# A Fourier filter and a two-layer network in one kernel: a table loaded with its negated columns, filter pieces cut elsewhere, and a last block that ends in parts

## The chip, the cores and the metric

The kernel runs on one core of a Trainium2 chip. The time is device microseconds of one execution; three runs of the kernel before gave 795.63, 795.70 and 795.91 us, median 795.7. One more execution was profiled.

The engines are TensorE (PE, matmuls; PEld its weight loads), VectorE (DVE), ScalarE (ACT), GpSimd (POOL) and SyncE (SP). DMAs are issued by instructions of SP, POOL or ACT and run beside the engines.

## The reference

```python
X = np.fft.rfft(x, axis=1)                 # x: 8 samples, 3008 positions, 256 channels
Y = X * (filt_r + 1j * filt_i)[None]       # 1505 frequencies, 256 channels
y = np.fft.irfft(Y, n=3008, axis=1)
h = y.reshape(24064, 256) @ w_in           # 256 x 2048
g = np.maximum(h, 0) + alpha * np.minimum(h, 0)
out = g @ w_out                            # 2048 x 256
```

## The kernel before

**The transform.** 3008 = 47 x 64, and the transform of a sample goes through in pieces. Piece a is a transform of length 47; then the data are turned; piece b multiplies by a table of twiddles (`twf_s`) for two of 24 frequencies k1 at a time (kp = 0 to 11 takes k1 = 2 kp and 2 kp + 1), VectorE multiplies the result by the filter (`filt_s`, L288 for sample 0), piece c multiplies by the inverse table (`twi_s` and `twx_s`), ScalarE or VectorE evicts to `v`; after another turn piece d ends in `yT`, the input of the network.

**Sample 0** has nothing to run beside, and is a class of its own (`First`). Its turns are done on PE (`turn_at`, L276, and `piece_t`, L312). Its piece b makes two products of 128 columns each per k1, from columns 64 to 192 and 0 to 128 of the table. The table `twf_s` in SBUF has 192 columns per k1; the constant in memory has 128, and the third part (128 to 192) is the first one negated, made on the chip by `third` (L327 on ScalarE, L329 on VectorE) for six k1 at a time. The two inverse tables have 128 partitions each, of which one half is loaded by SP (`load_twi`) and the other half is copied from it by POOL (`both_halves`, L341 and L342). `twx_s` lies in the last three buffers of `gtb`.

**POOL's order in sample 0** is written out by hand: the 8 loads of x, table columns for k1 0 to 6 (L332), filter pieces 0 to 4 (four DMAs, L142 and L146 for the real and the imaginary part), table 6 to 12, filter 4 to 10, table 12 to 18, filter 10 to 17, halves 0 to 4, table 18 to 24, filter 17 to 24, halves 4 to 8 and 8 to 12, the weights `win_s`, halves 12 to 18 and 18 to 24, the weights `wout_s`, the x of sample 1. POOL's DMAs share eight semaphores in turn, and a DMA is issued when the one eight places before it has landed.

**PE's order in sample 0**: for each kp, piece b of kp + 2, `turn_at` of kp + 4, piece c of kp - 2 (and 7, 8 and 9, 10 and 11 at the end). Piece b writes one of two PSUM buffers (`hps`), piece c one of two others (`op`).

**The network** runs in 48 blocks of 512 (some 384) positions, 16 steps each. A step j makes two matmuls of `up` (L452), on odd steps ScalarE evicts (L458) and VectorE makes the leaky rectifier (L461, L462) into a pair of `g`; beside it the same step makes `down` matmuls (L471) of the block before: 64 per block, row group by row group (128 positions, 16 matmuls of 256 columns each). After two row groups ScalarE evicts (L476) and SP stores (L434). The transforms of samples 1 to 7 are put between the steps by a plan of step numbers. The last block has no successor, so its 64 `down` matmuls run alone at the end.

Of the kernel before, what the change touches and what calls it, by code (L numbers as in the profile page):

```python
# [11 lines left out]
FP32 = mybir.dt.float32  # L12
# [3 lines left out]
N2 = 64  # L16
NK1 = 24
D = 256
# [14 lines left out]
AF = mybir.ActivationFunctionType  # L33
OP = mybir.AluOpType


def _build_consts():

    s1 = np.arange(N1)
    s2 = np.arange(N2)
    k1 = np.arange(NK1)
    p = np.arange(64)
    k2 = np.where(p < 32, p, 95 - p)
    g = np.where(p < 32, 1.0, -1.0)

    a1 = 2 * np.pi * np.outer(s1, k1) / N1  # L50
    wf1 = np.zeros((2 * N1, 96))
    wi3 = np.zeros((96, 2 * N1))
    scale = np.where(k1 == 0, 1.0, 2.0) / NFFT
    for h in range(2):
        r = slice(h * N1, h * N1 + N1)
        wf1[r, h * 48 : h * 48 + NK1] = np.cos(a1)
        wf1[r, h * 48 + NK1 : h * 48 + 48] = -np.sin(a1)
        wi3[h * NK1 : h * NK1 + NK1, r] = (np.cos(a1) * scale).T
        wi3[48 + h * NK1 : 48 + h * NK1 + NK1, r] = (-np.sin(a1) * scale).T

    kk = k1[:, None] + 47 * k2[None, :]
    ang = 2 * np.pi * s2[:, None, None] * kk[None, :, :] / NFFT
    c, s = np.cos(ang), np.sin(ang)
    twf = np.empty((128, NK1, 128))
    twf[:64, :, 64:], twf[64:, :, 64:] = c, s
    twf[:64, :, :64], twf[64:, :, :64] = -s * g, c * g
    ec, es = c.transpose(2, 1, 0), s.transpose(2, 1, 0)
    gp = g[:, None, None]
    twi = np.empty((128, NK1, 128))
    twi[:64, :, :64], twi[:64, :, 64:] = ec, es  # L70
    twi[64:, :, :64], twi[64:, :, 64:] = -es * gp, ec * gp
    return wf1, wi3, twf, twi
# [3 lines left out]
def kernel(  # L76
# [9 lines left out]
):  # L86
    nc = tc.nc
    wf1_np, wi3_np, twf_np, twi_np = _build_consts()
    wf1_d = nc.inline_tensor(wf1_np.astype(np.float16), name="c_wf1")
    wi3_d = nc.inline_tensor(wi3_np.astype(np.float16), name="c_wi3")  # L90
    twf_d = nc.inline_tensor(twf_np.astype(np.float16), name="c_twf")
# [10 lines left out]
    p_osb = ctx.enter_context(tc.tile_pool(name="p_osb", bufs=3))  # L102
    psH = ctx.enter_context(tc.tile_pool(name="psH", bufs=2, space=bass.MemoryType.PSUM))
    psO = ctx.enter_context(tc.tile_pool(name="psO", bufs=2, space=bass.MemoryType.PSUM))
# [9 lines left out]
    twf_s = konst.tile([128, NK1, 192], FP16, name="twf_s")  # L114
    twi_s = konst.tile([128, NK1, 128], FP16, name="twi_s")
# [7 lines left out]
    wout_s = konst.tile([128, 16, D], FP16, name="wout_s")  # L123
# [3 lines left out]
    twx_s = gtb[:, 14:17].rearrange("p a b c -> p (a b c)").rearrange("p (k m) -> p k m", m=128)  # L127
# [12 lines left out]
    def load_filt(dst, pbase, src, ka, kb):  # L140
        n = kb - ka
        nc.gpsimd.dma_start(  # L142
            out=dst[pbase : pbase + 32, ka:kb],
            in_=bass.AP(tensor=src.tensor, offset=src.offset + ka * D,
                        ap=[[47 * D, 32], [D, n], [1, D]]))
        nc.gpsimd.dma_start(  # L146
            out=dst[pbase + 32 : pbase + 64, ka:kb],
            in_=bass.AP(tensor=src.tensor, offset=src.offset + (N1 - ka) * D,
                        ap=[[47 * D, 32], [-D, n], [1, D]]))
# [171 lines left out]
    nc.sync.dma_start(out=wi3_s, in_=wi3_d.ap())  # L321
    make_identity(nc, id32)

    def third(eng, ka, kb):
        o, i = twf_s[:, ka:kb, 128:192], twf_s[:, ka:kb, 0:64]
        if eng is nc.scalar:
            nc.scalar.activation(o, i, AF.Copy, scale=-1.0)  # L327
        else:
            nc.vector.tensor_scalar(o, i, -1.0, None, OP.mult)  # L329

    def load_twf(ka, kb):
        nc.gpsimd.dma_start(out=twf_s[:, ka:kb, 0:128], in_=twf_d.ap()[:, ka:kb])  # L332

    def load_twi(ka, kb, ev):
        ev(twi_s[0:1, ka, 0:1], id16[0:1, 0:1])
        ev(twx_s[64:65, ka, 0:1], id16[64:65, 0:1])
        nc.sync.dma_start(out=twi_s[0:64, ka:kb], in_=twi_d.ap()[0:64, ka:kb])
        nc.sync.dma_start(out=twx_s[64:128, ka:kb], in_=twi_d.ap()[64:128, ka:kb])

    def both_halves(ka, kb):  # L340
        nc.gpsimd.tensor_copy(twi_s[64:128, ka:kb], twi_s[0:64, ka:kb])  # L341
        nc.gpsimd.tensor_copy(twx_s[0:64, ka:kb], twx_s[64:128, ka:kb])  # L342

    def load_g(ka, kb):
        load_filt(filt_s, 0, filt_r, ka, kb)
        load_filt(filt_s, 64, filt_i, ka, kb)

    load_twf(0, 6)
    load_g(0, 4)
    load_twf(6, 12)  # L350
    load_g(4, 10)
    load_twf(12, 18)
    load_g(10, 17)

    def warm(n):
        pw = psO.tile([128, 2, D], FP32, name="op")
# [11 lines left out]
            load_twi(4, 12, on_act)  # L368
    alp = psO.tile([128, 2, D], FP32, name="op")
    nc.tensor.transpose(alp[:, 0, 0:16], al16, id32)  # L370
    third(nc.scalar, 0, 6)
    f0.turn_at(0, on_act)
    f0.turn_at(1, on_dve)
    nc.vector.tensor_copy(al_s, alp[:, 0, 0:16])
# [1 line left out]
    f0.piece_b(0)  # L376
    f0.turn_at(2, on_act)
    f0.piece_b(1)
    both_halves(0, 4)
    load_twf(18, 24)  # L380
    load_g(17, 24)
    both_halves(4, 8)
    both_halves(8, 12)
    for kt in range(2):
        nc.gpsimd.dma_start(out=win_s[:, kt], in_=moe_w_in[kt * 128 : (kt + 1) * 128])
    third(nc.scalar, 6, 12)
    f0.turn_at(3, on_act)
    for kp in range(12):
        if kp < 10:
            if kp in (3, 6):  # L390
                third(nc.vector, 2 * kp + 6, 2 * kp + 12)
            f0.piece_b(kp + 2)
        if kp < 8:
            f0.turn_at(kp + 4, on_act)
        if kp == 0:
            load_twi(12, 24, on_act)
            both_halves(12, 18)
            both_halves(18, 24)
        for k in {9: (7, 8), 10: (9, 10), 11: (11,)}.get(kp, (kp - 2,) if kp > 1 else ()):
            f0.piece_c(k, on_dve if k == 10 else on_act)  # L400
    for q in range(2):
        nc.gpsimd.dma_start(
            out=wout_s[:, 8 * q : 8 * q + 8],
            in_=moe_w_out[1024 * q : 1024 * q + 1024].rearrange("(j p) d -> p j d", p=128))
# [15 lines left out]
    for p in range(NB // 2):  # L420
        t = 0
# [1 line left out]
            blocks.append((p, t, tn, 2 * p + (n >= 6)))  # L423
            t += tn

    def store(p, t0, osb, lane):
        t = t0
        while t < t0 + 128:
            b, r = 2 * p + t // NFFT, t % NFFT
            blk, o = r // 376, r % 376  # L430
            n = min(t0 + 128 - t, 376 - o)
            g, h = blk // 2, blk % 2
            row = b * NFFT + (o // 8) * N2 + NH * h + 8 * g
            nc.sync.dma_start(  # L434
                out=bass.AP(tensor=out.tensor, offset=out.offset + row * D,
                            ap=[[N2 * D, n // 8], [D, 8], [1, D]]),
                in_=osb[t - t0 : t - t0 + n, lane])
            t += n

    turn = [0]  # L440
# [1 line left out]
    class Block:  # L442
# [22 lines left out]
        def down(self, q):  # L465
            n = self.tn // 128
            for w in range(n * q, n * (q + 1)):
                si, k = w // 16, w % 16
                if si % 2 == 0 and k == 0:
                    self.op = psO.tile([128, 2, D], FP32, name="op")  # L470
                nc.tensor.matmul(self.op[:, si % 2], self.gts[k][:, 128 * si : 128 * si + 128],  # L471
                                 wout_s[:, k], start=(k == 0), stop=(k == 15))
                if k == 15 and (si % 2 == 1 or si == n - 1):
                    m = si % 2 + 1
                    osb = p_osb.tile([128, 2, D], FP32, name="osb")
                    nc.scalar.activation(osb[:, 0:m], self.op[:, 0:m], AF.Copy)  # L476
                    for lane in range(m):
                        store(self.p, self.t0 + 128 * (si - m + 1 + lane), osb, lane)

    plan = {}  # L480

# [36 lines left out]
    for b in range(3, NB):  # L518
        p = 96 * (b - 1)
# [19 lines left out]
    prev = None  # L539
    step = 0  # L540
    for p, t0, tn, _ in blocks:
# [6 lines left out]
                prev.down(j)  # L548
            step += 1
        prev = blk  # L550
    for q in range(16):
        prev.down(q)
    assert not plan


# [28 lines left out]
```

## Time and profile before

| | |
|---|---|
| median of three runs | 795.7 us |
| the profiled execution | 795.17 us |
| its span, first to last instruction | 793.4 us |
| PE, DVE, ACT, POOL busy | 97%, 78%, 75%, 25% |
| TensorE clock granted | 1.00 |
| first matmul of the network (L452) | 37.91 us |
| last matmul of the last block ends | 788.74 us |

Timeline rows read: start, length, engine, line, operation, tiles, shapes, count, and in brackets the idle time before and what ended it. Rows of the chain are start, length, what. Rows of the table by stretches are the stretch, its length, then busy time of PE, PEld, DVE, ACT and POOL with counts, the clock, the DMA share and GB/s. Times are in us from the start of the span.

### The profile page before, as it was taken

How to read it: one execution, taken by the hardware profiler on the slowest of the kernel's cores; microseconds unless marked ns; L12 is line 12 of the kernel's file. 1: busy time of each engine (PE TensorE's matmuls, PEld its weight loads, DVE VectorE, ACT ScalarE, POOL GpSimd, SP SyncE). 2: the span in 40 equal slices, each digit the busy share in tenths (PEclk: the TensorE clock that was granted, in tenths of full speed). 3: DMA queues.
4: the chain of work that ended last, by engine and by line, in shares of the span. 5: the costliest groups of instructions: out<-in, count | busy, mean ns of one | idle time of the engine just before them, and what ended most of it. 6: DMA issues, size and time to landing. Idle time of an engine off the chain costs nothing.

```text
span 793.4 us, 16044 instructions
## 1 busy us (share of the span) xinstructions
PE 773.1 (97%) x5908; PEld 538.5 (68%) x5908; DVE 619.8 (78%) x1368; ACT 597.9 (75%) x841; POOL 198.3 (25%) x275
## 2 busy tenths in 40 slices
PE   6899999999999999999999999999999999999997
PEld 6756656666676666766667666766667666766665
DVE  4787985788788787888787877887878888777773
ACT  4688778878778887788768887688867777787663
POOL 7710441153123221341223311242212222000000
PEclk9999999999999999999999999999999999999999
DMA  9995557685676648474684657656484333511111
GB/s 174 188 205 157 113 111 177 197 163 129 149 174 112 137 104 212 103 146 100 149 192 80 135 121 165 155 106 138 104 201 100 66 79 81 138 37 28 42 40 53
DMA packets 102517, 100.37 MB, mean 127 GB/s; under 512 B 11352, under 2 KB 92904, under 8 KB 102312
## 3 DMA queue, kind: packets, MB, share of 16 engines
q1 hardware_dynamic: 79992, 69.59, 33.2%
q0 software_dynamic: 22448, 29.77, 24.1%
q8 instruction: 46, 0.75, 0.4%
q14 instruction: 31, 0.25, 0.1%
HBM read 55.67 MB, written 46.66 MB: 129 GB/s over the span
## 4 chain that ended last, share of the span: by engine, by line
PE 88%; ACT 3%; DMA 3%; POOL 1%; DVE 1%; issue 1%; SPq 0%; ACTq 0%; POOLq 0%; DVEq 0%
PE hps L452 39%; PE op L471 39%; PE psF L175 3%; PE psF L236 3%; PE psF L214 2%; PE psF L195 2%; ACT gtb L458 2%; DMA twf_s<-c_twf 1%; DMA uu<-ww 1%; DMA filt_s<-in_filt_i_dram 1%; PE psF L312 1%; ACT asb L243 1%; POOL xs L137 1%; DMA zt<-v_dram 0%; DVE m L461 0%
## 5 line engine op out<-in xcount | busy, mean ns | idle before, releaser
L458 ACT ACTIVATE gtb<-hps 128x1024 f16<-128x1024 f32 (+1 forms) x384 | 385.3, 1004 | 133.4 <-PE hps L452 128.7
L471 PE MATMUL op<-wout_s,gtb 128*128 128x256 f16 x3008 | 451.1, 272 | 0.6 <-DVE gtb L462 0.6
L452 PE MATMUL hps<-yT,win_s 128*128 128x512 f16 (+1 forms) x1536 | 449.2, 374 | 0.4 <-ACT gtb L458 0.2
L471 PEld LDWEIGHTS <-gtb 128*128 128x128 f16 x3008 | 293.3, 98 | 189.5 <-DVE gtb L462 0.9
L461 DVE TENSOR_SCALAR m<-gtb,alm_s 128x512 f16<-128x512 f16 (+1 forms) x768 | 235.4, 349 | 126.7 <-ACT gtb L458 124.2
L462 DVE TENSOR_TENSOR gtb<-gtb,m 128x1024 f16<-128x1024 f16 (+1 forms) x384 | 261.6, 681 | 20.2 <-PE hps L452 0.5
L201 POOL DMA_DIRECT2D uu<-ww x168 | 140.3, 976 | 444.4 <-PE hps L452 307.9
L452 PEld LDWEIGHTS <-win_s 128*128 128x128 f16 x1536 | 145.2, 98 | 30.9 <-issue 3.1
L243 ACT ACTIVATE asb<-psF 96x512 f16<-96x512 f32 x112 | 66.2, 591 | 11.5 <-PE psF L175 11.4
L243 ACT ACTIVATE yT<-psF 128x376 f16<-128x376 f32 x120 | 57.1, 485 | 13.2 <-PE psF L236 12.7
L476 ACT ACTIVATE osb<-op 128x512 f32<-128x512 f32 x96 | 56.2, 585 | 6.1 <-issue 3.2
L198 DVE TENSOR_TENSOR ww<-psF,filts_s 128x512 f16<-128x512 f32 x84 | 57.4, 684 | 0.0
L243 ACT ACTIVATE v<-psF 128x512 f16<-128x512 f32 x84 | 49.4, 596 | 10.6 <-PE psF L214 9.8
L199 DVE TENSOR_TENSOR uu<-psF,filt_s 128x512 f16<-128x512 f32 x84 | 57.2, 681 | 0.0
L137 POOL DMA_DIRECT2D xs<-in_x_dram x64 | 44.4, 974 | 20.0 <-PE psF L175 14.0
L175 PE MATMUL psF<-xs,wf_s 94*96 94x512 f16 x112 | 42.7, 381 | 1.5 <-ACT v L243 0.9
L236 PE MATMUL psF<-wi_s,zt 96*128 96x94 f16 x504 | 40.3, 204 | 1.8 <-DMA zt<-v_dram 0.9
L236 PEld LDWEIGHTS <-zt 96*128 96x128 f16 x512 | 34.3, 97 | 6.1 <-issue 1.5
L214 PE MATMUL psF<-uu,twi_s 128*128 128x256 f16 x168 | 31.3, 273 | 2.3 <-DMA uu<-ww 1.3
L195 PE MATMUL psF<-at,twf_s 128*128 128x256 f16 x168 | 32.1, 272 | 0.3 <-ACT asb L243 0.2
L214 PEld LDWEIGHTS <-twi_s 128*128 128x128 f16 x168 | 15.7, 98 | 6.1 <-issue 2.0
L195 PEld LDWEIGHTS <-twf_s 128*128 128x128 f16 x168 | 15.8, 98 | 2.6 <-DVE uu L199 0.4
(59 smaller groups left out, 177.2 us busy)
## 6 DMA issues: line engine op xcount, KB each, us to landing
out_dram<-osb SPq DMA_DIRECT2D x128, 128.0 KB
xs<-in_x_dram POOLq DMA_DIRECT2D x64, 188.0 KB, 5.6
a_dram<-asb SPq DMA_DIRECT2D x28, 384.0 KB
uu<-ww POOLq DMA_DIRECT2D x168, 64.0 KB, 2.9
v_dram<-v SPq DMA_DIRECT2D x112, 96.0 KB
zt<-v_dram SPq DMA_DIRECT2D x28, 384.0 KB
at<-a_dram SPq DMA_DIRECT2D x20, 384.0 KB
at<-a_dram SPq DMA_DIRECT2D x32, 96.0 KB
```

The lines of the kernel that those rows point to most:

```text
L175: nc.tensor.matmul(ps[0:96], wf1_s, xs[:, o : o + 512], start=True, stop=True)
L195: nc.tensor.matmul(px[:, kh], twf_s[:, k1, 64:192], self.at[:, k1], start=True, stop=True)
L198: nc.vector.tensor_mul(ww, px, filts_s[:, 2 * kp : 2 * kp + 2])
L201: nc.gpsimd.dma_start(out=uu[o : o + 64], in_=ww[64 - o : 128 - o], accum_op=OP.add)
L214: nc.tensor.matmul(pv[:, kh], twi_s[:, k1], u[:, kh], start=u is us[0], stop=u is us[-1])
L236: nc.tensor.matmul(ps[:, m], self.zt[:, 8 * g + 4 * mh + m, dh * 128 : dh * 128 + 128], wi3_s, start=True, stop=True)
L243: nc.scalar.activation(o, i, AF.Copy)
L452: nc.tensor.matmul(self.hps[:, j % 2, 0:tn], win_s[:, kt, j * 128 : (j + 1) * 128], yT[:, kt, self.t0 : self.t0 + tn], start=(kt == 0), st ...
L458: nc.scalar.activation(g[:, :, 0:tn], self.hps[:, :, 0:tn], AF.Copy)
L461: nc.vector.tensor_scalar(m[:, i, 0:tn], g[:, i, 0:tn], 0.0, a, OP.min, OP.mult)
L462: nc.vector.tensor_add(g[:, :, 0:tn], g[:, :, 0:tn], m[:, :, 0:tn])
L471: nc.tensor.matmul(self.op[:, si % 2], self.gts[k][:, 128 * si : 128 * si + 128], wout_s[:, k], start=(k == 0), stop=(k == 15))
```

## The change

The constant of the forward table gets 192 columns, with the negated part in it, and each of the four table loads writes all of them; `third` and its four calls are gone. The filter pieces, cut at 4, 10 and 17 before, are cut at 4, 10, 16 and 20: the piece 16 to 20 is loaded ahead of the table for 18 to 24, the piece 20 to 24 behind it. The halves 4 to 8 are copied by VectorE, ahead of piece b of kp = 5, and no longer by POOL. The last block's `down` becomes `finish`: row groups 0 and 1 make their first 14 matmuls each, then their last two, into one PSUM tile; row group 2 and the two column halves of row group 3 accumulate in tiles of their own, are evicted by VectorE, and the first half of row group 3 is stored by ScalarE's queue, the rest by SP's.

```diff
-    twf = np.empty((128, NK1, 128))
-    twf[:64, :, 64:], twf[64:, :, 64:] = c, s
+    twf = np.empty((128, NK1, 192))
+    twf[:64, :, 64:128], twf[64:, :, 64:128] = c, s
     twf[:64, :, :64], twf[64:, :, :64] = -s * g, c * g
+    twf[:, :, 128:] = -twf[:, :, :64]
...
-    def third(eng, ka, kb):
-        o, i = twf_s[:, ka:kb, 128:192], twf_s[:, ka:kb, 0:64]
-        if eng is nc.scalar:
-            nc.scalar.activation(o, i, AF.Copy, scale=-1.0)
-        else:
-            nc.vector.tensor_scalar(o, i, -1.0, None, OP.mult)
-
     def load_twf(ka, kb):
-        nc.gpsimd.dma_start(out=twf_s[:, ka:kb, 0:128], in_=twf_d.ap()[:, ka:kb])
+        nc.gpsimd.dma_start(out=twf_s[:, ka:kb], in_=twf_d.ap()[:, ka:kb])
...
-    def both_halves(ka, kb):
-        nc.gpsimd.tensor_copy(twi_s[64:128, ka:kb], twi_s[0:64, ka:kb])
-        nc.gpsimd.tensor_copy(twx_s[0:64, ka:kb], twx_s[64:128, ka:kb])
+    def both_halves(eng, ka, kb):
+        eng.tensor_copy(twi_s[64:128, ka:kb], twi_s[0:64, ka:kb])
+        eng.tensor_copy(twx_s[0:64, ka:kb], twx_s[64:128, ka:kb])
...
-    load_g(10, 17)
+    load_g(10, 16)
...
-    third(nc.scalar, 0, 6)
     f0.turn_at(0, on_act)
...
-    both_halves(0, 4)
+    both_halves(nc.gpsimd, 0, 4)
+    load_g(16, 20)
     load_twf(18, 24)
-    load_g(17, 24)
-    both_halves(4, 8)
-    both_halves(8, 12)
+    load_g(20, 24)
+    both_halves(nc.gpsimd, 8, 12)
...
-    third(nc.scalar, 6, 12)
     f0.turn_at(3, on_act)
     for kp in range(12):
         if kp < 10:
-            if kp in (3, 6):
-                third(nc.vector, 2 * kp + 6, 2 * kp + 12)
+            if kp == 3:
+                both_halves(nc.vector, 4, 8)
             f0.piece_b(kp + 2)
...
-    def store(p, t0, osb, lane):
+    def store(p, t0, osb, lane, eng=nc.sync, ca=0, cb=D):
...
+        def finish(self):
+            def down(acc, si, k, first, ca=0, cb=D):
+                nc.tensor.matmul(acc, self.gts[k][:, 128 * si : 128 * si + 128], wout_s[:, k, ca:cb],
+                                 start=first, stop=(k == 15), skip_group_check=True)
+
+            op = psO.tile([128, 2, D], FP32, name="op")
+            osb = p_osb.tile([128, 2, D], FP32, name="osb")
+            for ks in (range(14), range(14, 16)):
+                for si in range(2):
+                    for k in ks:
+                        down(op[:, si], si, k, si == 0 and k == 0)
+            nc.scalar.activation(osb, op, AF.Copy)
+            for lane in range(2):
+                store(self.p, self.t0 + 128 * lane, osb, lane)
+            osb = p_osb.tile([128, 2, D], FP32, name="osb")
+            parts = ((0, 0, 256, nc.sync), (1, 0, 128, nc.scalar), (1, 128, 256, nc.sync))
+            accs = [psH.tile([128, 2, 512], FP32, name="hps")[:, 0] for _ in range(2)]
+            accs.insert(0, psO.tile([128, 2, D], FP32, name="op")[:, 0])
+            for (lane, ca, cb, eng), acc in zip(parts, accs):
+                acc = acc[:, 0 : cb - ca]
+                for k in range(16):
+                    down(acc, 2 + lane, k, k == 0, ca, cb)
+                nc.vector.tensor_copy(osb[:, lane, ca:cb], acc)
+                store(self.p, self.t0 + 256 + 128 * lane, osb, lane, eng, ca, cb)
...
-    for q in range(16):
-        prev.down(q)
+    prev.finish()
```

More of the change, by code (lines that the diff above doesn't have):

```diff
@@ L396 @@
             load_twi(12, 24, on_act)
-            both_halves(12, 18)
-            both_halves(18, 24)
+            both_halves(nc.gpsimd, 12, 18)
+            both_halves(nc.gpsimd, 18, 24)
         for k in {9: (7, 8), 10: (9, 10), 11: (11,)}.get(kp, (kp - 2,) if kp > 1 else ()):
@@ L433, in store @@
             row = b * NFFT + (o // 8) * N2 + NH * h + 8 * g
[L434 to L437, printed above, removed]
+            eng.dma_start(
+                out=bass.AP(tensor=out.tensor, offset=out.offset + row * D + ca,
+                            ap=[[N2 * D, n // 8], [D, 8], [1, cb - ca]]),
+                in_=osb[t - t0 : t - t0 + n, lane, ca:cb])
             t += n
```

## The prediction

> **What bounds the kernel now.** I read the page's busy times first, then the table by stretches, then the chain of work that ended last at its two ends, then the timelines of the engines that it names.
>
> ```profile
> PE 773.1 (97%) x5908; PEld 538.5 (68%) x5908; DVE 619.8 (78%) x1368; ACT 597.9 (75%) x841; POOL 198.3 (25%) x275
> ```
> ```profile
> 400.00:600.00 200.00, 200.00 (x1490) 138.62 (x1489) 162.62 (x363) 156.52 (x218) 52.03 (x68) 1.00 0.64 141
> ```
>
> In the middle TensorE (PE, the first number behind the length) has no idle time at all, so no edit that leaves its work alone can be felt there; whatever is saved ahead of it or behind it shifts the whole. The change touches only the two ends: the first 35 us, where sample 0 goes through its transform, and the last 13 us. The chain through the first end:
>
> ```profile
> 5.82 7.93 DMA twf_s<-c_twf
> ...
> 21.90 5.86 DMA filt_s<-in_filt_i_dram
> ...
> 29.03 1.22 DVE gtb L288
> 30.30 0.61 PE hps L284 x4
> ...
> 31.02 0.06 PE op L300
> 31.07 0.06 PE op L301
> ...
> 31.40 0.60 ACT v L243
> ```
>
> POOL's queue of loads comes first, then the last filter piece (issued at 21.90, landed at 27.76), then VectorE's products of L288, then the c pieces and their evictions. VectorE shows what the filter costs:
>
> ```profile
> 15.14 0.69 DVE L246 CAST at<-psF 128x512 f16<-128x512 f32 x1 [0.66 <-PE psF L276]
> 15.75 0.17 DVE L374 COPY al_s<-op 128x16 f32<-128x16 f32 x1
> 16.33 5.76 DVE L288 TENSOR_TENSOR gtb<-hps,filt_s 128x1024 f16<-128x1024 f32 x5 [0.21 <-PE hps L284]
> 22.01 0.25 DVE L329 TENSOR_SCALAR twf_s<-twf_s 128x384 f16<-128x384 f16 x1
> 22.62 3.53 DVE L288 TENSOR_TENSOR gtb<-hps,filt_s 128x1024 f16<-128x1024 f32 x3 [0.36 <-DMA filt_s<-in_filt_i_dram]
> 27.88 4.62 DVE L288 TENSOR_TENSOR gtb<-hps,filt_s 128x1024 f16<-128x1024 f32 x4 [1.53 <-PE op L301]
> ```
>
> Twelve products (I number them by kp, 0 to 11) run 1.15 us apart. Product 8 stands idle 1.53 us. The row names a PE event at that moment, but the chain has the filter landing at 27.76; product 8 takes frequencies 16 and 17, and 17 is in the piece that lands then. That hole is the first thing the change can fill.
>
> **The start, POOL first.** POOL issues every table and filter load and makes the halves, in order:
>
> ```profile
> 14.03 0.51 POOL L142 DMA_DIRECT2D filt_s<-in_filt_i_dram  x1 [0.40 <-DMA twf_s<-c_twf]
> 14.53 0.56 POOL L146 DMA_DIRECT2D filt_s<-in_filt_i_dram  x1
> 17.54 0.62 POOL L146 DMA_DIRECT2D filt_s<-in_filt_i_dram  x1
> 18.20 0.60 POOL L341 COPY twi_s<-twi_s 64x512 f16<-64x512 f16 x1
> 19.42 0.86 POOL L332 DMA_DIRECT2D twf_s<-c_twf  x1
> 20.27 0.54 POOL L142 DMA_DIRECT2D filt_s<-in_filt_r_dram  x1
> 20.79 0.61 POOL L146 DMA_DIRECT2D filt_s<-in_filt_r_dram  x1
> 21.90 0.62 POOL L146 DMA_DIRECT2D filt_s<-in_filt_i_dram  x1
> 22.57 0.60 POOL L341 COPY twi_s<-twi_s 64x512 f16<-64x512 f16 x1
> 23.90 0.61 POOL L341 COPY twi_s<-twi_s 64x512 f16<-64x512 f16 x1
> 25.13 1.15 POOL L385 DMA_DIRECT2D win_s<-in_moe_w_in_dram  x2
> 26.32 0.82 POOL L341 COPY twi_s<-twi_s 64x768 f16<-64x768 f16 x1
> 27.20 0.82 POOL L342 COPY gtb<-gtb 64x768 f16<-64x768 f16 x1
> ```
>
> The table load now writes 192 columns in one run per partition in place of 128 columns in six runs. Its issue is 0.86; one run per partition should cost what a plain load costs, 0.51 (14.03) to 0.62 (21.90): I take 0.55, so 0.3 less each. Its bytes grow by half. Bounds of its transfer: nothing (longer runs make up for the bytes), or half of what 192 KB take at the 217 GB/s of a row of the end below, 0.9, so +0.45. I take +0.1, nearer to nothing, since six runs per partition become one. The instruction at 14.03 waits for that first load; so it starts at 14.15. Ahead of the first copy of halves lies one more table load (-0.3): that copy starts at 18.0 (was 18.20). Two copies, 1.22 (18.20 to 19.42): 19.25. Four new issues for frequencies 16 to 20, as in 20.27 to 22.57, 2.3: 21.5. The last table load, 0.55: 22.1. Four issues for 20 to 24: 24.4. The halves 8 to 12, 1.23 (23.90 to 25.13): 25.6. Weights, 1.19: 26.8. Halves 12 to 18, 1.70: done at 28.5 against 28.02. So POOL gains 1.33 by the copies it hands over (22.57 to 23.90), loses 2.3 by four more issues, and ends 0.5 later. Each issue also waits for the landing of the eighth before it, as at 14.03; the last of the new pieces by that needs the first of 16 to 20 landed, by 23.7, which I take as just met.
>
> VectorE: the first product could start 0.2 sooner without the ScalarE negation ahead of it, but product 2 needs the filter piece 4 to 10, which landed at 18.4 (second row below), and it ran at 16.33 + 2.30 = 18.63, so I count nothing. Product 4 ends at 22.1. Then come the two copies that move to VectorE, 64x512 each. Their bounds are 0.25 (128x384, the negation at 22.01, which goes) and 0.69 (15.14, though from PSUM); I take 0.31, nearest to the negation scaled by columns. Product 5 starts at 22.7 (was 22.62), product 7 ends at 26.25. When is product 8's filter there?
>
> ```profile
> filt_s<-in_filt_i_dram POOLq DMA_DIRECT2D x1, 112.0 KB, 5.0
> filt_s<-in_filt_i_dram POOLq DMA_DIRECT2D x1, 96.0 KB, 3.9
> twf_s<-c_twf POOLq DMA_DIRECT2D x1, 192.0 KB, 5.6
> ```
>
> These answer for one issue each: the last column is the time from issue to landing, 5.0 for the issue at 17.54, 3.9 for that at 14.53 and 5.6 for the table load at 19.42; the issue at 21.90 took 5.86. The last issue of 16 to 20 starts near 20.9: landing 24.8 to 26.8. I take 25.7, before 26.25: product 8 runs at 26.25 and its 1.53 us hole is gone. What is late next: product 9 needs the last table load (issue 21.5 + 5.6 = 27.1) and one piece b on PE:
>
> ```profile
> 26.52 0.60 PE L284 MATMUL hps<-at,twf_s 128*128 128x256 f16 x4
> 29.16 0.61 PE L284 MATMUL hps<-at,twf_s 128*128 128x256 f16 x4 [1.37 <-DVE gtb L288]
> ```
>
> 27.1 + 0.6 = 27.75, against 29.03 now: -1.3. Product 10: filter 20 to 24, last issue 23.8 + 5.0 = 28.8, just at its turn (27.75 + 1.15 = 28.9). PE meanwhile: piece b of 10 at 28.35, then c of 6, which needs the halves 12 to 18 at 28.5, to 29.25; then b of 11 at 29.25 against 30.30 in the chain. From there the chain is c, eviction, c, unchanged (c goes at 0.06 a matmul). The start gives **1.05, say 1.1 us**; bounds 0 and 1.8 (all of the 1.53 and a negation of 0.25).
>
> A rule speaks against giving copies to VectorE. The row at 22.01 ran its 0.25 us inside POOL's issue of 21.90, which took 0.62 where its like at 20.79 (0.61) had no such neighbour: neither was held up. The Trainium skill, "SBUF — State Buffer", section "Who interferes with whom", says that a VectorE copy in a two-port mode and GpSimd share one port pair, and that the second to come is blocked until the first is done. By that rule POOL could lose 0.6 more, the start would give 0.5 and the time would be 793.4. The trace does not show it, so the sum leaves it out.
>
> **The end.** Rows of PE, ScalarE and SP:
>
> ```profile
> 780.39 2.13 PE L471 MATMUL op<-wout_s,gtb 128*128 128x256 f16 x18
> 783.11 5.63 PE L471 MATMUL op<-wout_s,gtb 128*128 128x256 f16 x50 [0.60 <-DVE gtb L462]
> 788.83 0.60 ACT L476 ACTIVATE osb<-op 128x512 f32<-128x512 f32 x1 [2.90 <-PE op L471]
> ```
> ```profile
> 785.96 1.10 SPq L434 DMA_DIRECT2D out_dram<-osb  x2
> 789.45 1.22 SPq L434 DMA_DIRECT2D out_dram<-osb  x2
> ```
> ```profile
> 791.50:792.00 0.50, 0.00 (x0) 0.00 (x0) 0.00 (x0) 0.00 (x0) 0.00 (x0) 1.00 0.76 217
> 792.00:792.50 0.50, 0.00 (x0) 0.00 (x0) 0.00 (x0) 0.00 (x0) 0.00 (x0) 1.00 0.01 4
> ```
>
> The last block's 64 matmuls wait 0.60 for the last pair of g, because all 16 of row group 0 come first. With 14 of group 0 and 14 of group 1 ahead, the pair (there at 783.1) is wanted at 780.83 + 28 x 0.109 = 783.9: no wait. (0.109 is 5.63 less one matmul's 0.27, over 49.) Then 4 and 16 more, and 32 matmuls of half width, at the 0.06 that L300 and L301 take for 128 columns: PE ends at 780.39 + 52 x 0.109 + 32 x 0.057 + 0.16 = 788.05 (0.16 for the end of the last one), against 788.74: **-0.7**. The last eviction is 128 columns on VectorE in place of 512 on ScalarE: between 0.17 (16 columns, 15.75) and 0.69 (512, 15.14), by columns 0.28, against 0.60: **-0.3**. Behind it one SP issue in place of two (1.22): **-0.6**; SP is free for it: the first half is evicted by 780.83 + 32 x 0.109 + 0.1 + 0.6 = 785.0, 0.9 sooner than the 785.96 at which its three issues begin now, and the store of row group 2 goes out in between. The last store has 64 KB in place of 128; data flows until 792.0 now, and half of it less is worth 0 to 0.3: **-0.2**. ScalarE's own issue of the other half (ready at 787.5, nothing queued behind it) is 0.9 us ahead and hidden. Sum **1.8 us**, bounds 1.3 and 2.1.
>
> The profiled execution took 795.17 with a span of 793.4, 0.53 under the median of 795.7. By its own time 795.17 - 1.1 - 1.8 = 792.3; on the median **792.8 us**.
>
> **The rivals.**
>
> *POOL takes the place of the filter wait.* Four more issues, each tied to a landing eight issues earlier; if the piece that the last issue waits for lands 1 us later than 23.7, the halves 12 to 18 come at 29.5 and piece c of 6 holds PE until b of 11 stands where it does now. Start 0, end 1.8: 793.9. For it: POOL has no idle time from 14.03 on. Against: the landings that precede are not moved by the change.
>
> *The heavier table pushes everything behind it.* At +0.45 for each load, the filter 4 to 10 lands 0.9 later, product 2 slips to 19.3 and product 7 ends near 27.0; the last table load, 0.35 more for each of four loads, lands at 28.5, and product 9 runs at 29.1, where it runs now. Start 0, so again 793.9. Against: the six short runs per partition are gone.
>
> *The split does not split.* If product 8 still waits for all of 16 to 24, it runs at 28.8 and not 27.88, and the start loses 0.9: 794.8. Against it: product 5 at 22.62 ran while 17 to 24 was still in flight, so waits go by the piece.
>
> *Slower: ScalarE's first transfer.* No row shows a DMA that ScalarE issues. If its store from 787.5 - 1.1 = 786.4 takes as long to land as the slowest issue of this trace (7.93, in the chain), it lands at 794.3, 1.9 us after the last store of now (792.4): 797.6. It decides once it takes longer than 6 us. Against: SP's last store, issued at 790.1 (the second of the two from 789.45), has no data left to move at 792.0 and has landed by about 792.4.
>
> **How the numbers follow.** About 0.2%, 1.6 us, is what a measurement of this kernel can tell from no change. Forecast 0.62, POOL 0.17, heavy table 0.08, no split 0.07, slower 0.06. Faster than 794.1: the forecast and two thirds of POOL and heavy table, 0.79; within: the other third and no split, 0.15; slower 0.06. The range from 791.4 (1.8 and 2.1, with 0.4 for what one profiled run can be off) to 794.4 (POOL's case with the end at its lower bound) leaves out the last two and the edges, under 0.2.
>
> **What would show it.** Start right: no idle time over 0.3 us before product 8, b of 11 near 29.2, first L452 matmul near 36.8 (now 37.9). POOL's rival: a PE matmul of L301 released by POOL for over 0.5 us. End right: no wait for g in the last matmuls, last matmul near 786.9 (now 788.74), under 3.8 us from it to the end (now 4.7). Wrong: a filter landing after 28.9, or the end set by ScalarE's store.

## The result, and the profile after

Run side by side with the kernel before, the changed kernel takes 793.25 us (median of 8 runs, 791.52 to 794.03) against 795.25 (8 runs, 794.59 to 795.91). The ratio is 0.9972 [0.9961, 0.9983], that is 2.2 us less, between 1.4 and 3.1. The profiled execution took 793.11 us, with a span of 791.3. For the short kernels E5 to E10 below, runs over 1.5% above the fastest run of the same kernel are left out of the medians.

**The start.** The lines moved: products are L289, piece b is L285, the first `up` is L444, the copies of halves L335 and L336, the table load L326. VectorE's timeline of the changed kernel (start, length, engine, line, operation, tiles, shape, count, idle time before):

```profile
17.28 6.05 DVE L289 TENSOR_TENSOR gtb<-hps,filt_s 128x1024 f16<-128x1024 f32 x5 [0.29 <-PE hps L285]
23.36 0.29 DVE L335 COPY twi_s<-twi_s 64x512 f16<-64x512 f16 x1
23.68 0.37 DVE L336 COPY gtb<-gtb 64x512 f16<-64x512 f16 x1
24.07 8.01 DVE L289 TENSOR_TENSOR gtb<-hps,filt_s 128x1024 f16<-128x1024 f32 x7
```

The hole of 1.53 us before product 8 is gone: from 17.28 to 32.08 VectorE has no idle time that the view names. But the products begin at 17.28 and not at 16.33. POOL's rows fell nearly where the sum put them:

```profile
14.18 0.49 POOL L143 DMA_DIRECT2D filt_s<-in_filt_i_dram  x1 [0.70 <-DMA twf_s<-c_twf]
15.22 0.57 POOL L326 DMA_DIRECT2D twf_s<-c_twf  x1
...
20.76 0.55 POOL L147 DMA_DIRECT2D filt_s<-in_filt_i_dram  x1
...
23.97 0.61 POOL L335 COPY twi_s<-twi_s 64x512 f16<-64x512 f16 x1
...
27.59 0.82 POOL L336 COPY gtb<-gtb 64x768 f16<-64x768 f16 x1 [0.46 <-DMA gtb<-c_twi]
```

The wider table load costs 0.57 to issue; the filter piece 16 to 20 is fully issued by 21.31 (20.76 + 0.55) and, by the trace's record of that DMA, landed 4.8 us behind the start of its issue, at 25.6; the halves 12 to 18 are done at 28.41. Why the products began late is seen in PE's stretch from 13 to 20 us, of before first and then of the changed kernel (length, busy time of PE, PEld, DVE, ACT, POOL, then the granted clock, DMA share, GB/s):

```profile
13.00:20.00 7.00, 5.35 (x66) 4.32 (x66) 5.64 (x9) 4.97 (x13) 6.43 (x11) 1.00 1.05 210
```
```profile
13.00:20.00 7.00, 6.74 (x56) 5.61 (x54) 4.67 (x8) 3.18 (x7) 6.19 (x12) 0.51 1.08 236
```

In this execution TensorE was granted half its clock for nearly all of these 7 us (a mean of 0.51, against 1.00): fewer matmuls took more busy time. PE's timeline shows the cost, one piece b at 1.01 where it takes 0.60 otherwise, and the later marks:

```profile
16.23 1.01 PE L285 MATMUL hps<-at,twf_s 128*128 128x256 f16 x4 [0.26 <-ACT at L244]
...
29.88 0.61 PE L285 MATMUL hps<-at,twf_s 128*128 128x256 f16 x4
...
37.50 0.61 PE L444 MATMUL hps<-yT,win_s 128*128 128x512 f16 x2
```

So piece b of 11 stands at 29.88 (30.30 before) and the network starts at 37.50 (37.91 before): 0.4 earlier in this execution.

**The end.** The timelines of PE, VectorE, ScalarE's queue and SP's queue in the changed kernel:

```profile
780.33 5.40 PE L474 MATMUL op<-wout_s,gtb 128*128 128x256 f16 x48
785.57 1.95 PE L474 MATMUL hps<-wout_s,gtb 128*128 128x128 f16 x32
```
```profile
787.55 0.29 DVE L494 COPY osb<-hps 128x128 f32<-128x128 f32 x1 [0.60 <-PE hps L474]
```
```profile
786.98 0.66 ACTq L426 DMA_DIRECT2D out_dram<-osb  x1
```
```profile
786.85 1.42 SPq L426 DMA_DIRECT2D out_dram<-osb  x1
788.37 0.55 SPq L426 DMA_DIRECT2D out_dram<-osb  x1
```

The last block's matmuls, 48 of full and 32 of half width for the 64 of before, run without a break and end at 787.52 (785.57 + 1.95): 7.19 us after the first of them, against 7.91 before (780.83 to 788.74). The last copy takes 0.29 and is done at 787.84. But SP is still busy with the issue for row group 2, which took 1.42 us, so the last store is issued at 788.37 and not at 787.84. From the last matmul to the end are 3.8 us (791.3 - 787.52); before it was 4.7. In this execution the two ends thus give 0.4 and 0.7 + 0.9, all but 0.1 of the 2.1 us by which the spans differ (793.4 and 791.3).

### The profile page after: what moved, and what is told of

Its sections match the earlier page's. It is cut to its first block, busy times and chain, and to the rows that moved or that the text cites. A ratio compares the mean times of both kernels' runs of the same rounds, so it can differ in the third digit from the quotient of the medians.

```text
span 791.3 us, 16085 instructions
## 1 busy us (share of the span) xinstructions
PE 774.7 (98%) x5924; PEld 540.4 (68%) x5924; DVE 621.6 (79%) x1371; ACT 596.6 (75%) x838; POOL 197.5 (25%) x277
## 4 chain that ended last, share of the span: by engine, by line
PE 90%; ACT 3%; DMA 3%; DVE 2%; issue 1%; POOL 1%; SPq 0%; ACTq 0%; POOLq 0%
PE hps L444 39%; PE op L463 38%; PE psF L176 3%; PE psF L237 3%; PE psF L215 2%; PE psF L196 2%; ACT gtb L450 2%; DMA uu<-ww 1%; DMA xs<-in_x_dram 1%; PE hps L285 1%; PE op L474 1%; PE psF L313 1%; ACT asb L244 1%; POOL xs L138 0%; DMA zt<-v_dram 0%
## 5 line engine op out<-in xcount | busy, mean ns | idle before, releaser
L444 PE MATMUL hps<-yT,win_s 128*128 128x512 f16 (+1 forms) x1536 | 449.2, 374 | 0.4 <-ACT gtb L450 0.2
L463 PE MATMUL op<-wout_s,gtb 128*128 128x256 f16 x2944 | 443.9, 272 | 0.0
L463 PEld LDWEIGHTS <-gtb 128*128 128x128 f16 x2944 | 287.1, 98 | 188.0
L444 PEld LDWEIGHTS <-win_s 128*128 128x128 f16 x1536 | 145.3, 98 | 31.2 <-issue 3.3
```

What stands on the lines that cost most here:

```text
L444: nc.tensor.matmul(self.hps[:, j % 2, 0:tn], win_s[:, kt, j * 128 : (j + 1) * 128], yT[:, kt, self.t0 : self.t0 + tn], start=(kt == 0), st ...
```

## The experiments

The runs come in three groups, each with runs of the kernel before beside it: E1 to E4 with 29 runs of before (median 795.37), E5 to E8 with 11 (795.1), E9 to E12 with 17 (795.44). A ratio is to the runs of before in the same group, with its 95% interval.

**E1, the start alone.** The changed kernel with the old end:

```diff
-    prev.finish()
+    for q in range(16):
+        prev.down(q)
```

> The change's start with the old end. Theory CLOCK (the start's edits are worth about 1.1 us, but in the profiled run of the changed kernel the granted clock was 0.5 from 13 to 20 us, which put the first product at 17.28 in place of 16.33 and ate about 0.7 of it): 0.4 to 1.1 us faster than before, by whether the profile shows the clock at 1.00; with the clock at 1.00 the first network matmul (L444) starts near 36.8, with it at 0.5 near 37.5. Rival EDITS (the whole-table load or the handed-over copies themselves delay the first product, the clock is a bystander): 0.4 us faster whatever the clock, first network matmul near 37.5. Both: the end as before, 4.7 us from the last matmul to the end.

Measured: 795.51 (11 runs, 794.29 to 797.9), ratio 1.0000 [0.9991, 1.0009]. In its profile (VectorE, then PE) the start looks as forecast:

```profile
16.68 2.36 DVE L289 TENSOR_TENSOR gtb<-hps,filt_s 128x1024 f16<-128x1024 f32 x2
19.50 3.48 DVE L289 TENSOR_TENSOR gtb<-hps,filt_s 128x1024 f16<-128x1024 f32 x3 [0.46 <-issue]
...
23.33 0.29 DVE L336 COPY gtb<-gtb 64x512 f16<-64x512 f16 x1
23.65 8.01 DVE L289 TENSOR_TENSOR gtb<-hps,filt_s 128x1024 f16<-128x1024 f32 x7
```
```profile
37.07 0.61 PE L444 MATMUL hps<-yT,win_s 128*128 128x512 f16 x2
```

No idle time before product 8, the network from 37.07, a span of 792.5. But that execution, 794.29, is the fastest of its 11, and the median shows no gain at all, give or take 0.7 us.

**E2, the end alone.** The kernel before with the new end (`finish`, and `store` with its queue and columns):

```diff
-    for q in range(16):
-        prev.down(q)
+    prev.finish()
```

> The kernel before with the new end alone. From the changed kernel's profile: 0.8 us off the last matmul and 0.9 off what follows it, so 1.7 us faster than before (793.5 against 795.25), and the first network matmul at 37.9 as before if the clock is 1.00 there. If CLOCK holds, a profile of this kernel too may show 0.5 between 13 and 20 us, since nothing in the start differs from before; if EDITS holds, it shows 1.00 as before's does. In the SP queue the store of row group 2 takes about 1.4 us to issue beside ScalarE's issue, as in the changed kernel.

Measured: 793.93 (11 runs, 792.41 to 795.15), ratio 0.9982 [0.9973, 0.9991]: 1.4 us less, between 0.7 and 2.1. Its profile, VectorE and PE at the start, PE and SP's queue at the end:

```profile
22.60 0.56 DVE L329 TENSOR_SCALAR twf_s<-twf_s 128x384 f16<-128x384 f16 x1
...
27.34 4.62 DVE L288 TENSOR_TENSOR gtb<-hps,filt_s 128x1024 f16<-128x1024 f32 x4 [0.22 <-DMA filt_s<-in_filt_i_dram]
```
```profile
37.37 0.61 PE L452 MATMUL hps<-yT,win_s 128*128 128x512 f16 x2
```
```profile
785.39 1.95 PE L482 MATMUL hps<-wout_s,gtb 128*128 128x128 f16 x32
```
```profile
786.67 0.59 SPq L434 DMA_DIRECT2D out_dram<-osb  x1
787.69 0.55 SPq L434 DMA_DIRECT2D out_dram<-osb  x1
```

Here the issue for row group 2 took 0.59, the last one went out as soon as its data were there, and from the last matmul (787.34) to the end of the span (790.6) are 3.3 us: 1.4 less than before. With the 0.7 of the matmuls the rows give 2.1. This execution, 792.41, is the fastest of its 11. The other reading is in the old start: the same hole that was 1.53 in the profile before is 0.22 here, and the network starts at 37.37, not 37.91. The hole varies from execution to execution, and part of it only changes its name: here the second negation, ahead of product 8, took 0.63 in place of 0.28, so from the end of product 7 to product 8 are 0.78 us (26.56 to 27.34), against 1.73 before (26.15 to 27.88).

**E3, the changed kernel with its clock kept up.** More filler matmuls (`warm`) between the parts of piece a, so that PE does not stand idle before 13 us:

```diff
-            warm((16, 6, 5, 8)[i // 4])
+            warm((22, 18, 20, 8)[i // 4])
```

> The changed kernel with more idle-filling matmuls on PE between the chunks of piece a (22, 18, 20, 8 in place of 16, 6, 5, 8), enough to fill PE's waits for the chunks of x at 8.7, 10.3 and 12.1 us and no more. CLOCK, and that the halving follows PE's idle time before it: clock 1.00 from 13 to 20, first product at 16.1 to 16.4, first network matmul near 36.8, 0.5 to 0.9 us faster than the changed kernel and less scatter between runs. EDITS: first product still at 17.2, no gain. If the halving is not caused by idle time: clock 0.5 in some stretch again.

Measured: 793.53 (7 runs, 792.4 to 796.25), ratio 0.9981 [0.9967, 0.9994]. The stretch from 13 to 20 us, and VectorE's product 2:

```profile
13.00:20.00 7.00, 5.31 (x65) 4.25 (x65) 5.01 (x8) 4.42 (x11) 5.98 (x12) 1.00 1.14 240
```
```profile
19.31 3.49 DVE L289 TENSOR_TENSOR gtb<-hps,filt_s 128x1024 f16<-128x1024 f32 x3 [0.67 <-issue]
```

The clock is whole and the network starts at 36.89, yet the time is not below the 793.25 of the changed kernel as it is. So a whole clock did not bring the missing gain. That alone does not clear the clock, because the filler has a price of its own (E4). Part of what the lowered clock costs is paid anyway: with a whole clock product 2 stands 0.67 before it runs.

**E4, the same filler in the kernel before.** The same diff.

> The kernel before with the same additional idle-filling matmuls. Its profile had the clock at 1.00 throughout, so CLOCK expects no more than the share of its runs in which the clock is halved: 0 to 0.4 us faster (in before product 8's wait for the filter at 27.76 hides most of a late first product). EDITS: no change. If the additional matmuls delay piece a: 0.2 to 0.6 us slower, first product after 16.6.

Measured: 797.04 (11 runs, 795.05 to 798.43), ratio 1.0020 [1.0011, 1.0029], 1.6 us slower. The clock was whole here too, but the filter piece was late:

```profile
28.58 3.49 DVE L288 TENSOR_TENSOR gtb<-hps,filt_s 128x1024 f16<-128x1024 f32 x3 [1.25 <-DMA filt_s<-in_filt_i_dram]
```

The piece landed at 28.46 (27.76 before) and the network started at 38.61. Its last issue had waited 0.37 us for the landing of the load eight places before it, so it began at 22.01 (21.90 before), and then took 6.45 us to land (5.86). Why more matmuls on PE should go with slower loads was not found out. What follows is only that the filler isn't free, and that E3's comparison has the same flaw.

**E5 to E8, the start in a short kernel.** To see the start without 750 us behind it, the network is cut to its first block and the transforms of samples 1 to 7 are left out, so 47 of 48 blocks are missing. E5 is the kernel before so cut, and E8 the one with the whole new start:

```diff
+    blocks = blocks[:1]
...
-    assert not plan
```

> The kernel before with the network cut after its first block of 512 positions (the other 47 blocks and the other seven transforms are left out), so that little but the start is left in the time: the yardstick for the next three. About 65 us of span (the first block ends near 56 us in the full kernel, 64 matmuls take 7 us, then the stores). First network matmul between 37.4 and 38.6, as in the profiles so far with this start; scatter of spans under 1.5 us if the scatter of the full kernel comes from its middle, as large as there (2 to 3 us) if it comes from the start.

E6 adds the 192-column table alone:

```diff
-        nc.gpsimd.dma_start(out=twf_s[:, ka:kb, 0:128], in_=twf_d.ap()[:, ka:kb])
+        nc.gpsimd.dma_start(out=twf_s[:, ka:kb], in_=twf_d.ap()[:, ka:kb])
...
-    third(nc.scalar, 0, 6)
```

> The same cut, with the whole-table load alone added (192 columns loaded, no negation; filter pieces at 4, 10, 17 and all copies on POOL as before). Theory SHIFT (the prediction's sum holds for an undisturbed start): no wait ends sooner, 0.2 us faster to 0.2 slower. Rival HEAVY (half more bytes push the filter pieces back): 0.4 to 0.9 us slower, last filter landing near 28.3 instead of 27.3 to 27.8.

E7 adds the split at 16 and 20 to it; the copies 4 to 8 stay on POOL:

```diff
-    load_g(10, 17)
+    load_g(10, 16)
...
+    load_g(16, 20)
     load_twf(18, 24)
-    load_g(17, 24)
+    load_g(20, 24)
```

> The same cut, whole table and the filter pieces at 4, 10, 16 and 20, all copies still on POOL. SHIFT: product 8 no longer waits, but POOL makes four more issues (2.3 us) and keeps its copies, so the halves 12 to 18 are ready near 29.8 and hold piece c of kp 6: 0.2 slower to 0.4 us faster than before's cut. Rival NOTHING (the wait that the split removes is short in most executions): within 0.2 of the table's cut, and no wait on POOL's copies over 0.3.

E8 moves these copies to VectorE as well:

```diff
-    both_halves(nc.gpsimd, 4, 8)
...
+            if kp == 3:
+                both_halves(nc.vector, 4, 8)
```

> The same cut with the change's whole start (table, split, the halves 4 to 8 on VectorE). SHIFT: 0.8 to 1.1 us faster than before's cut, of which the copies give the larger half. NOTHING: 0 to 0.4 us faster. CLOCK (the granted clock falls to 0.5 for some 7 us in a part of the runs, with either start): within each of the four cuts the runs with a mean clock under 0.97 are 0.5 to 1 us longer, and the share of such runs is the same for all four within chance.

Measured, medians: E5 65.16 (4 runs, 64.56 to 65.43), E6 64.51 (4, 64.32 to 65.10), E7 64.70 (3, 64.43 to 65.18), E8 64.18 (4, 64.05 to 64.68); of all runs 65.31 (6, up to 67.31), 65.10 (7, up to 66.82), 65.76 (6, up to 67.29) and 64.18. By these the whole start gives 1.0 to 1.1 us, and the table alone, or table and split, between 0.7 and -0.5. But the times hold more than the start. The last 50 matmuls of the only block, which the start does not touch, in E5 and then in E6:

```profile
51.61 5.63 PE L473 MATMUL op<-wout_s,gtb 128*128 128x256 f16 x50 [0.86 <-DVE gtb L464]
```
```profile
52.21 7.30 PE L463 MATMUL op<-wout_s,gtb 128*128 128x256 f16 x50 [0.86 <-DVE gtb L454]
```

E8 and E9 have the 5.63 too, E7 and E10 the 7.30, and in these and in E6 the clock from 50 to 60 us is 0.83 (0.99 to 1.00 in the others). A fall of the clock at that place is worth 1.67 us, more than any of the differences sought, and how many runs of each kernel had it is not known. E5 and E8 can be compared as profiled, both without that fall: the network starts at 37.34 and 36.97, and the spans are 62.8 and 62.2, so the whole start gives 0.4 to 0.6 in these two executions, with E8's clock lowered at its start.

The profiled executions of E6 and E7 were the longest of theirs (66.82 and 67.29); whether the others show their waits is not known. VectorE's product 8 in E5 and E6, product 7 in E7, and a line of PE's waits in E7:

```profile
27.32 4.62 DVE L288 TENSOR_TENSOR gtb<-hps,filt_s 128x1024 f16<-128x1024 f32 x4 [1.07 <-PE psF L276]
```
```profile
27.97 3.49 DVE L289 TENSOR_TENSOR gtb<-hps,filt_s 128x1024 f16<-128x1024 f32 x3 [1.69 <-DMA filt_s<-in_filt_i_dram]
```
```profile
27.30 4.62 DVE L289 TENSOR_TENSOR gtb<-hps,filt_s 128x1024 f16<-128x1024 f32 x4 [1.83 <-PE hps L285]
```
```profile
PE op L301 <- POOL twi_s L335: 1.4, 1, 1.4
```

In E6 the filter wait stays. In E7 the filter is no longer what is waited for, but PE waits 1.4 us for POOL's copy: four more issues stand ahead of the halves 4 to 8 on POOL. Piece c of 2 holds PE, and with it piece b and product 7. That is the first rival of the prediction, and in this execution it appears when the copies are not handed over. In E8, VectorE and the stretch:

```profile
23.54 8.01 DVE L289 TENSOR_TENSOR gtb<-hps,filt_s 128x1024 f16<-128x1024 f32 x7
```
```profile
13.00:20.00 7.00, 5.92 (x61) 4.88 (x60) 4.87 (x8) 3.77 (x9) 5.93 (x11) 0.76 1.14 254
```

No hole, and this although the clock was lowered in part of the stretch.

**E9, the copies alone**, in the short kernel (old table, old filter pieces):

```diff
-    both_halves(4, 8)
...
+            if kp == 3:
+                both_halves(4, 8, nc.vector)
```

> The cut kernel of before with only the halves 4 to 8 given to VectorE (table, negations and filter pieces as before). WHOLE (the start's gain needs the split and the copies together: the split empties the filter wait, the copies free POOL of what the split adds): 65.3 as before's cut, within 0.4, product 8 still idle about 0.5 us or more for the filter, which VectorE's two more copies only shorten. Rival COPIES (POOL's load is the limit in itself): about 64.2.

Measured: 65.90 (3 runs, 65.49 to 66.24; of all 5 runs 66.24). No cut kernel before was run in this group, so the time does not say whether the 65.3 that was expected holds. VectorE's rows, then POOL's of the same moment:

```profile
23.32 0.53 DVE L341 COPY twi_s<-twi_s 64x512 f16<-64x512 f16 x1
23.88 0.63 DVE L342 COPY gtb<-gtb 64x512 f16<-64x512 f16 x1
```
```profile
23.10 0.60 POOL L341 COPY twi_s<-twi_s 64x512 f16<-64x512 f16 x1
23.76 0.61 POOL L342 COPY gtb<-gtb 64x512 f16<-64x512 f16 x1
```

The copies that take 0.29 and 0.37 in the changed kernel take 0.53 and 0.63 here. Each ends 0.14 or 0.15 after the POOL copy that runs beside it (23.85 after 23.70, 24.51 after 24.37). E2's negation of 0.56 in place of 0.25 does the same: it ends at 23.16, and the POOL copy beside it at 23.04. In all of these POOL's copy began first. In E5 VectorE is ahead by 0.01, and there its negation takes the usual 0.25 and POOL's copy 0.70 in place of 0.60:

```profile
22.35 0.25 DVE L329 TENSOR_SCALAR twf_s<-twf_s 128x384 f16<-128x384 f16 x1
```
```profile
22.36 0.70 POOL L341 COPY twi_s<-twi_s 64x512 f16<-64x512 f16 x1
```

In the changed kernel VectorE's first copy, at 23.36, stands beside a DMA issue of POOL, and takes 0.29. Beside a DMA issue the hold is smaller, and goes to either side: E11's second copy on VectorE, with POOL's issue, and E1's issue on POOL beside the copy at 23.33:

```profile
22.85 0.41 DVE L336 COPY gtb<-gtb 64x512 f16<-64x512 f16 x1
```
```profile
22.58 0.56 POOL L147 DMA_DIRECT2D filt_s<-in_filt_r_dram  x1
```
```profile
23.12 0.60 POOL L143 DMA_DIRECT2D filt_s<-in_filt_i_dram  x1
```

The copy takes 0.12 more than 0.29 and ends 0.12 after the issue; the issue takes 0.1 more than the usual 0.50 and ends 0.1 after the copy. The Trainium skill, "SBUF — State Buffer", section "Who interferes with whom", says that, of a VectorE copy in a two-port mode and GpSimd, the one that comes second is blocked until the other's instruction is done. Copy against copy the rows agree on who is held up: 0.24 to 0.35 us are lost on VectorE in E9 and E2, 0.1 on POOL in E5. Copy against issue they lose 0.1 and not the whole instruction.

Product 8 stands idle no longer in E9, but only because the products ahead of it are late: it runs at 28.29, where it ran at 27.32 in E5. In this execution the clock was lowered from 13 to 20 us (0.76) and the first product ran at 17.54 (15.97 in E5), so the missing hole cannot be put down to the copies.

**E10, split and copies without the wide table**, in the short kernel:

```diff
-    load_g(10, 17)
+    load_g(10, 16)
...
+    load_g(16, 20)
...
-    load_g(17, 24)
-    both_halves(4, 8)
+    load_g(20, 24)
...
+            if kp == 3:
+                both_halves(4, 8, nc.vector)
```

> The cut kernel of before with the split and the copies, but the table loaded in 128 columns with the negations on ScalarE and VectorE. WHOLE: between before's cut and the whole start, 64.4 to 65.0: the two negations on VectorE (0.25 each) and 0.3 us more for each table issue on POOL come back. Rival TABLE (the whole table is what matters): about 65.3. Rival NO TABLE COST (the negations lie in idle time): 64.2.

Measured: 65.73 (4 runs, 65.14 to 66.02), above the 64.4 to 65.0 that was expected. Only E9, in the same group, compares with it directly: 0.2 less, which the scatter of either covers. The profiled execution, 65.74, is one with the 1.67 us at its end. VectorE's product 8:

```profile
26.87 4.60 DVE L288 TENSOR_TENSOR gtb<-hps,filt_s 128x1024 f16<-128x1024 f32 x4
```

The hole is gone without the table, and the network starts at 36.88, in the range of the whole start (36.72 to 37.07 at a whole clock). By position, in this one execution, the gain of the start is that of split and copies together; the time of the table's part stays unclear.

**E11, the start alone once more**, the same kernel as E1 in another group:

> The full kernel with the start alone once more, to narrow the start's worth in the full time. SHIFT: 1.1 us faster than before, as the cut kernels (64.18 against 65.31). Rival ABSORBED (the waits of PE between 80 and 150 us take an earlier start back): 0 to 0.3 us faster, and PE's waits for uu and zt there sum to 1 us more than before's 2.2.

Measured: 795.42 (11 runs, 794.04 to 796.26), ratio 0.9997 [0.9988, 1.0005]: between 1.0 less and 0.4 more, so a gain of 1.1 lies outside. PE's first `up`, and PE's waits from 14 to 150 us (total, times, longest), first of E11, then of the kernel before:

```profile
36.72 0.61 PE L444 MATMUL hps<-yT,win_s 128*128 128x512 f16 x2
```
```profile
PE psF L215 <- DMA uu<-ww: 1.1, 3, 0.7
PE psF L237 <- DMA zt<-v_dram: 1.0, 1, 1.0
```
```profile
PE psF L214 <- DMA uu<-ww: 1.3, 3, 0.7
PE psF L236 <- DMA zt<-v_dram: 0.9, 1, 0.9
```

In this execution nothing takes the gain back: the waits for later loads sum to 2.1 and to 2.2, and from the first eviction of the network to the last pass 741.23 us, against 741.21 before. Its span is 792.3, 1.1 less than before. But 794.04 is again the fastest of its 11, and 22 runs of E1 and E11 together have a median span of 793.65, where 57 runs of before have 793.6. Nor does the lowered clock hide a gain of 1.1: those of the 22 with a mean clock above 0.997 (12 runs) have a mean span of 793.5, those of the 57 (34 runs) 793.4.

**E12, the end on one queue.** The changed kernel with the first half of row group 3 on SP:

```diff
-            parts = ((0, 0, 256, nc.sync), (1, 0, 128, nc.scalar), (1, 128, 256, nc.sync))
+            parts = ((0, 0, 256, nc.sync), (1, 0, 128, nc.sync), (1, 128, 256, nc.sync))
```

> The changed kernel with all three stores of the second half of the last block on SP's queue. If the second queue is worth what its issue takes: SP issues the first half of row group 3 from 7.2 us after the start of the last eviction of g, 0.6 long, and the last half at once behind it, 0 to 0.2 us later than with two queues (in the profile of the end alone SP waited 0.4 us for VectorE there): 0 to 0.2 us slower than the changed kernel, the time from the last matmul to the end 3.3 to 3.5 us. Rival: two queues disturb each other (SP's issue took 1.42 us beside ScalarE's in the changed kernel's profile, 0.59 in the end alone): 0.3 us faster.

Measured: 793.59 (7 runs, 792.78 to 794.33), ratio 0.9973 [0.9962, 0.9984], the same as the changed kernel. SP's queue:

```profile
787.21 1.57 SPq L426 DMA_DIRECT2D out_dram<-osb  x1
788.88 0.55 SPq L426 DMA_DIRECT2D out_dram<-osb  x1
789.52 0.56 SPq L426 DMA_DIRECT2D out_dram<-osb  x1
```

The issue for row group 2 was long here too, 1.57, with no issue of ScalarE beside it; so it does not take a second queue to make it long. In this execution, with its long issue, both halves queue behind it and the end comes 4.5 us after the last matmul (792.4 - 787.88), 0.7 later than in the changed kernel. The times show no difference between one queue and two.

## Why the prediction was right, point by point

**The total: 792.8 forecast, 793.25 measured.** Of the two terms one held and one did not, in the time of the full kernel. That the total came so near is partly luck. The forecast took 2.9 us off 795.7, and 2.2 were measured; but the kernel before had a median of 795.25 beside the changed kernel, 0.45 lower. The end alone (1.4 in E2) with nothing from the start would also lie in the range, at 794.3 from 795.7.

**The end, 1.8 with bounds 1.3 and 2.1, held.** By itself it gives 1.4 [0.7, 2.1] in E2, and the rows give 1.6 in the changed kernel's profile and 2.1 in E2's. Term by term: the matmuls 0.72 (forecast 0.7), with no wait for g; the last eviction 0.29 (0.28 forecast); the smaller store 0.3 to 0.4, since from the last issue to the end are 2.9 us (791.3 - 788.37; E2 790.6 - 787.69) against 3.3 before (793.4 - 790.1), where 0.2 stood and 0.3 was the bound; and one issue less, 0.6, which came whole in E2 but not in the changed kernel's profile, where the issue ahead took 1.42 in place of 0.6 and gave 0.5 of it back. The prediction had "SP is free for it" and priced an SP issue only by its usual length. The slower rival, ScalarE's first transfer, did not come: its issue of 0.66 at 786.98 delays nothing, and the end follows SP's last store.

**The start, 1.1: right as a mechanism, not shown as a time in the full kernel.** Undisturbed, the steps fell where they were put: the table's issue 0.56 to 0.59 (0.55), POOL's instruction behind the first load at 14.18 (14.15), the filter 16 to 20 landed 25.6 (25.7), the halves 8 to 12 done at 25.25 (25.6) and 12 to 18 at 28.41 (28.5), piece b of 11 at 29.10 in E11 and 29.45 in E1 (29.25), the network from 36.72 and 37.07 (36.8). The split splits: in none of E8, E10, E11 and the changed kernel does product 8 stand idle. In the short kernel the two profiled executions that can be compared differ by 0.4 to 0.6; the 1.0 to 1.1 of the medians is mixed with the clock at the end of that kernel. In the full kernel the start changes the time by 0.0 us (E1) and -0.2 (E11), with intervals from -0.7 to +0.7 and from -1.0 to +0.4: a gain of 1.1 lies outside both.

The step that failed is the first one: the start was sized against the hole of 1.53 us in one profiled execution. The same old start shows 0.22 in E2, 1.07 in E5, 1.25 in E4 (with the filler). With the network's start at 37.37 (E2) and 37.34 (E5) as the old position, the new one (36.72 to 37.07 at a whole clock, 37.50 at half) is worth 0.3 to 0.65, or nothing; against the 37.91 from which the forecast was made it is 0.8 to 1.2. E2 and E5 were profiled in the fastest execution of theirs, so the usual old position may lie between. A gain of 0.3 to 0.65 would still fit the intervals of E1 and E11, and the 0.7 by which the changed kernel stands below E2 (793.93 - 793.25, not run side by side). That this is the whole reason is not shown: the profiled executions of E1 and E11 were the fastest of theirs, and where a median one loses its gain stays open.

**The rivals and the rule.** The heavier table does not push the filter: product 2's wait of 0.24 to 0.67 in the new start stands in the old one too (0.62 in E5's, 0.77 in E2's timeline), and was absent in the profile from which the forecast was made. The piece 4 to 10 lands 3.7 to 4.5 us after its last issue begins in the kernels with the wide table, and 3.6 to 4.8 in those with the old one. So the product-2 step, "I count nothing", rested on one execution. POOL's place as the wait came true where the copies stayed with it, in E7's one profile. And the rule on the shared port, which the sum left out at 0.6 for POOL, is there, but costs 0.1 here, because DMA issues of POOL and not its copies stand beside VectorE's copies.

## What to carry to other kernels

The size of a hole in front of one instruction in one profile need not be what it is worth: before pricing a change by it, see how far the same hole varies between executions, and when one profile is all there is, price it between nothing and its size. A load split off to arrive earlier costs issues on its queue, so move as much other work off that queue in the same edit, or the queue can become the wait. Cutting a kernel short to see its start brings its own end into the time, so compare positions and not only times. And when work goes to VectorE beside GpSimd, put it beside GpSimd's DMA issues, which cost 0.1 us here, and not behind its copies, which cost 0.24 to 0.35.

## What the hardware showed that was not expected

TensorE's granted clock is whole in most of every profile, and fell to half for a few us in some. From about 13 us the fall lasted 6.9 us in the changed kernel's profile (2 x 0.49 x 7, from the mean of 0.51) and 3.4 in E8's and E9's (from 0.76); at the end of E6, E7 and E10 it lasted 3.4 too (2 x 0.17 x 10, from the 0.83 of 50 to 60 us). The mean clock of the whole run was 0.997 or less in 23 of 57 runs of before, in 10 of 22 of E1 and E11, and in none of the 18 of E3 and E4, whose filler leaves PE little idle time before 13 us. (A mean of 0.998 can come from the end alone, where PE has no work left, as in E11's profile.) Yet in the changed kernel's profile the idle stretches before the fall are 0.8 us at most, and E11 kept its clock with no more PE work from 10 to 13 us (1.32 of 3 us busy, against 1.51). The Trainium skill, "TensorE: Matmul & The Clock Gate", section "Part 1: The HAM clock gate (the "warmup" mystery)", says that activity is judged over a window of about 3.4 us that runs free of the kernel. The lengths of 3.4 and 6.9 agree with that, and it would explain why the same kernel falls in one execution and not in the next, but no run here moves the window. What a fall costs depends on the place: 1.67 us on the 50 matmuls of E6, and less in the full kernel, where before's 34 runs with a mean clock above 0.997 have a mean span of 793.4 and the other 23 one of 794.0.

One SP issue of a 128 KB store took 1.42 us in the changed kernel's profile and 1.57 in E12's, but 0.59 in E2's: long with one store queue and with two, short with two. What lengthens it was not tried.
